# Sliding-window attention and an MLP on one core: two row blocks centred on ScalarE instead of VectorE, sums of W2 moved between periods, one transpose moved by a unit

## The chip, the core and the metric

The kernel runs on one core of a Trainium2 chip. Its engines work side by side, each through its own queue in order: TensorE (PE: matmuls and transposes, with weight loads as PEld), VectorE (DVE), ScalarE (ACT), GpSimd (POOL), and SyncE (SP), which here only issues transfers. The metric is the device time of one execution in microseconds (us); the runs shown before have a median of 311.74 us. "PSUM" is the memory that PE writes; it is handed out here in banks.

## What is computed

Eight batches, eight heads, 576 positions, head size 64. Attention looks back over 64 positions, and its output, put together over the heads (512 columns), goes through a layer norm, two matrix products with a relu between them, and a residual add:

```python
scores = scale * np.matmul(q, k.transpose(0, 1, 3, 2))
mask = (rel >= 0) & (rel < window)          # rel = row - column, window = 64
attn = softmax(np.where(mask, scores, -1e9))
x = matmul(attn, v), heads side by side      # (8, 576, 512)
xn = (x - mu) / np.sqrt(var + 1e-06) * g_ln
out = x + np.maximum(xn @ w_ch1, 0.0) @ w_ch2   # 512 x 2048, 2048 x 512
```

## The kernel before

**Groups.** The first 512 rows of each batch are a group (0 to 7) of four row blocks of 128; the last 64 rows of all batches make group 8. For each block the attention has these steps:

- `t_main` (L219) transposes q and k, on PE with a copy out of PSUM by ACT or DVE, from group 3 on q by a DMA of SP;
- `s_mm` (L260) multiplies them on PE and takes the exponential on ACT; `s_mask` (L295) applies the mask on DVE;
- `b_step` (L302) multiplies with v on PE (tile xps) and on DVE divides by the sum (L323, L326) and takes mean and variance (L328, L331); v is used in two alignments, vA and vB. From group 2 on vB is made by `make_vB` (L164) with two DMAs that POOL issues (L165, L166);
- `z_step` (L335) makes z, the centred block in half precision. For groups 0 and 1 it is called at the end of `b_step` and only subtracts the mean, on DVE (L341); the scale is applied after the MLP (`newton`, L367, and L417). For later groups POOL also applies the scale (L345 to L348);
- `zt_step` (L350) transposes z into zT, on PE with a copy by ACT (L360, L363) for groups 0 and 1 and for block 3 of groups 3 and 5, otherwise by a DMA of SP (L356).

**Periods and units.** The MLP of group g is one period of the loop at L823. `mlp_units` (L386) gives a list of units of PE work: first the product with W1 (`l1`, L392, 128x512 outputs, or `l1_half`, L526, half as wide), each ended by a relu on ACT, then the product with W2. In the periods of groups 0 and 1 the latter is done directly (`l2`, L403, four matmuls a unit, and in group 0 `l2_two`, L539, for its first two blocks), and `add_out` (L414) adds each finished block on DVE and stores it. The bank of such a block is one of two with the tag "mm", so the third block waits until the first has been added.

From group 2 on W2 is multiplied by Strassen's scheme in Winograd's form: seven products instead of eight (`product`, L450, in the order 1, 2, 6, 5, 7, 4, 3) of half-size blocks, into banks A, B and C. It needs four sums of the hidden activations in each period (`s_sums`, L435, DVE, tiles sS) and four sums of blocks of W2, made once (`w2_sums`, L705, DVE, tiles wT):

```python
o, x, y, op = {3: (t3, b22, b12, ALU.subtract), 2: (t2, t3, b11, ALU.add),
               4: (t4, b21, t2, ALU.subtract), 1: (b12, b12, b11, ALU.subtract)}[i]
nc.vector.tensor_tensor(out=o, in0=x, in1=y, op=op)
```

Number 1 overwrites the block b12 of W2 itself, so it must come behind group 1's products with W2 and behind T3. Each sum is called in two halves of 128x1024. `post` (L477) adds a bank to the block on DVE; product 6 goes on in bank A after product 1 has been added (L497), product 7 after that.

**The order.** It is written out by hand. `at(i, f, ...)` (L831) puts a step into slot i, and the step is issued behind unit i of the period; within a slot the order of the calls holds. Every engine runs its part of this list in order, so where a step stands sets what is queued behind it. Group g's period holds the attention of group g + 1: group 1's blocks 0 and 1 come in slots 18 and 21 of group 0's period (L850, L851), their transposes in slots 22 and 24 (L852, L853), which are the units of `l2_two` and the first of `l2`. The casts of W2 from f32 are POOL's (`w2_cast`, L203); they are issued before the loop and run as the loads land, some of which land in the tiles wT (L195). In group 1's period T3 stands in slots 25 and 28 (L881, L882), and in group 2's period T2, number 1 and T4 in slots 4 to 9 (L907 to L910), ahead of and among `b_step` of block 1 (slot 7), the mask of block 2 (slot 8) and the first halves of `s_sums` (slots 8 to 11).

Of the kernel before, what the change touches and what calls it, by code (L numbers as in the profile page):

```python
# [10 lines left out]
FP32 = mybir.dt.float32  # L11
# [3 lines left out]
AF = mybir.ActivationFunctionType  # L15
ALU = mybir.AluOpType
# [4 lines left out]
def kernel(  # L21
# [10 lines left out]
    nc = tc.nc  # L32
# [11 lines left out]
    scale = 1.0 / (D ** 0.5)  # L44
# [257 lines left out]
    def b_step(g, kb):  # L302
# [29 lines left out]
        if g < 2:  # L332
            z_step(g, kb)

    def z_step(g, kb):  # L335
        z = p_blk.tile([128, DM], FP16, tag="z", name=f"z_{g}_{kb}")
        zsd[(g, kb)] = z
        xv = x_norm[(g, kb // 2)][:, kb % 2, :]
        mu, var = mvg[g][:, kb, 0:1], mvg[g][:, kb, 1:2]
        if g < 2:  # L340
            nc.vector.tensor_scalar(out=z, in0=xv, scalar1=mu, scalar2=None, op0=ALU.subtract)  # L341
            return
        t = p_blk.tile([128, 3], FP32, tag="rsz", name=f"rsz_{g}_{kb}")
        ve, rs, nm = (t[:, i:i + 1] for i in range(3))
        nc.gpsimd.tensor_scalar(out=ve, in0=var, scalar1=1.0, scalar2=EPS, op0=ALU.mult, op1=ALU.add)  # L345
        nc.gpsimd.tensor_tensor(out=rs, in0=ve, in1=mhalf, op=ALU.pow)
        nc.gpsimd.tensor_scalar(out=nm, in0=mu, scalar1=rs, scalar2=-1.0, op0=ALU.mult, op1=ALU.mult)
        nc.gpsimd.tensor_scalar(out=z, in0=xv, scalar1=rs, scalar2=nm, op0=ALU.mult, op1=ALU.add)  # L348
# [474 lines left out]
    for g in range(NGRP):  # L823
        if g == NGRP - 1:
            for _ in rest:
                pass
            break
        units, s_sums = mlp_units(g, (8, 16)[g] if g < 2 else 0, g == 0, g > 1)
        slots = [[] for _ in range(len(units) + 1)]

        def at(i, f, *a):  # L831
            slots[min(i, len(slots) - 1)].append((f, a))

        b = g + 1
        if g == 0:
            at(0, b_step, 0, 3)
            at(1, zt_step, 0, 2)
            at(3, zt_step, 0, 3)
            at(4, newton, 0, 0, 4)
            at(11, t_main, 1, 0, 0, 1)  # L840
            at(12, t_main, 1, 1, 0, 1)
            at(13, vB_cur, 1, 0, 1)
            at(13, vB_prev, 1, 0, 1)
            at(13, vB_cur, 1, 1, 1)
            at(13, vB_prev, 1, 1, 1)
            at(16, s_mm, 1, 0)
            at(16, s_mask, 1, 0)
            at(17, s_mm, 1, 1)
            at(17, s_mask, 1, 1)
            at(18, b_step, 1, 0)  # L850
            at(21, b_step, 1, 1)  # L851
            at(22, zt_step, 1, 0)  # L852
            at(24, zt_step, 1, 1)  # L853
            at(26, t_main, 1, 0, 1, 0)
            at(27, t_main, 1, 1, 1, 1)
            at(28, vB_cur, 1, 2, 0)
            at(28, vB_prev, 1, 2, 1)
            at(29, vB_cur, 1, 3, 0)
            at(29, s_mm, 1, 2)
            at(29, s_mask, 1, 2)  # L860
            at(30, s_mm, 1, 3)
            at(30, s_mask, 1, 3)
            at(30, load_v, 2, 0, 4)
            at(33, b_step, 1, 2)
        if g == 1:
            at(0, cast_qk, 2, 0)
            at(0, cast_qk, 2, 1)
            at(1, b_step, 1, 3)
            at(2, zt_step, 1, 2)
            at(13, newton, 1, 0, 4)  # L870
            at(5, zt_step, 1, 3)
            at(4, alloc_v, 2)
            at(4, alloc_qkT, 2)
            at(4, alloc_vB, 2)
            at(5, cast_v, 2, 0, 4)
            at(5, make_vB, 2)
            at(4, t_main, 2, 0, 0)
            at(4, t_main, 2, 1, 0)
            at(6, t_main, 2, 0, 1)
            at(6, t_main, 2, 1, 1)  # L880
            at(25, w2_sums, 3, 0, 4)  # L881
            at(28, w2_sums, 3, 4, 8)  # L882
            for j in range(4):
                at((9, 13, 16, 19)[j], s_mm, 2, j)
                at((10, 14, 17, 20)[j], s_mask, 2, j)
                at((14, 17, 20, 23)[j], b_step, 2, j)
                at((14, 17, 20, 23)[j], z_step, 2, j)
                at((18, 21, 24, 27)[j], zt_step, 2, j)
            at(3, load_qk, 3, 0)
            at(4, load_qk, 3, 1)  # L890
            at(7, load_v, 3, 0, 4)
            at(8, alloc_qkT, 3)
            at(8, cast_qk, 3, 0)
            at(10, cast_qk, 3, 1)
            at(14, alloc_v, 3)
            at(14, cast_v, 3, 0, 2)
            at(14, cast_v, 3, 2, 4)
            at(17, alloc_vB, 3)
            at(17, make_vB, 3)
            at(31, s_mm, 3, 0)  # L900
            at(31, s_mask, 3, 0)
            for i, (x, half) in zip((12, 24, 12, 28), ((0, 0), (1, 0), (0, 1), (1, 1))):
                at(i, t_main, 3, x, half, 0)
            at(40, load_qk, 4, 0)
            at(40, load_qk, 4, 1)
            at(40, load_v, 4, 0, 4)
        if g == 2:  # L907
            for m, i in enumerate((2, 1, 4)):
                at(4 + 2 * m, w2_sums, i, 0, 4)
                at(5 + 2 * m, w2_sums, i, 4, 8)  # L910
        if g > 1 and g + 2 < B:
            at(11, alloc_qkT, g + 2)
            if g + 2 >= XQ:
                at(11, cast_qk, g + 2, 0, (0,))
                at(11, cast_qk, g + 2, 1, (0,))
                at(11, cast_qk, g + 2, 0, (1,))
            else:
                at(11, cast_qk, g + 2, 0)
        if g > 1 and b < B:
            for j in range(4):  # L920
                if j:
                    at((2, 7, 12)[j - 1], s_mm, b, j)
                    at((3, 8, 13)[j - 1], s_mask, b, j)
                at((2, 7, 12, 17)[j], b_step, b, j)
                at((2, 7, 12, 17)[j], z_step, b, j)
                at((12, 12, 18, 23 if b in (3, 5) else 22)[j], zt_step, b, j)
        for n, i in enumerate(TAILS.get(g, ())):
            ts = (10, 11, 14, 20) if n else (1, 2, 5, 11)
            at(ts[0], s_mm, NGRP - 1, i)
            at(ts[1], s_mask, NGRP - 1, i)  # L930
            at(ts[2], b_step, NGRP - 1, i)
            at(ts[2], z_step, NGRP - 1, i)
            at(ts[3], zt_step, NGRP - 1, i)
        n = g + 2
        if g > 1 and n < B:
            at(16, cast_qk, n, 1, (1,) if n >= XQ else (0, 1))
            at(20, alloc_v, n)
            at(20, cast_v, n, 0, 2)
            at(21, cast_v, n, 2, 4)
            at(21, alloc_vB, n)  # L940
            at(21, make_vB, n)
            for i, (x, half) in zip((13, 18, 13, 22) if g == 2 else (13, 17, 13, 21),
                                    ((0, 0), (1, 0), (0, 1), (1, 1))):
                at(i, t_main, n, x, half, 0)
            at(27, s_mm, n, 0)
            at(28, s_mask, n, 0)
            if n + 1 < B:
                at(40, load_qk, n + 1, 0)
                at(40, load_qk, n + 1, 1)
                at(40, load_v, n + 1, 0, 4)  # L950
        if g > 1:
            for i in range(1, 5):
                at(7 + i, s_sums, 0, 4, i)
                at(13 + i // 3, s_sums, 4, 6, i)
                at((15, 15, 19, 21)[i - 1], s_sums, 6, 8, i)
        for n, i in enumerate(TAILS.get(g + 1, ())):
            if n == 0:
                at(1, load_tail, i)
                at(24 if i < 2 else 18, cast_tail, i)
                at(27 if i < 2 else 22, t_tail, i, 0)  # L960
                at(29 if i < 2 else 22, t_tail, i, 1)
            else:
                at(25, load_tail, i)
        if len(TAILS.get(g, ())) == 2:
            at(3, cast_tail, TAILS[g][1])
            at(7, t_tail, TAILS[g][1], 0)
            at(8, t_tail, TAILS[g][1], 1)
        if g == NGRP - 2:
            at(0, w1_sums, 1, 2)
            at(3, w1_sums, 3)  # L970
            at(21, w1_sums, 4)
            at(24, z_sums, NGRP - 1, 1, 2)
            at(25, z_sums, NGRP - 1, 3, 4)
            at(27, begin_last)
        for i, u in enumerate(units):
            if g > 1 and i == 20:
                tbank["shared"] = True
            u()
            for f, a in slots[i]:
                f(*a)  # L980
        for f, a in slots[len(units)]:
            f(*a)
# [28 lines left out]
```

The softmax here doesn't subtract the row's maximum and nothing guards it: scores larger than these inputs give would overflow.

## Time and profile before

| | us |
|---|---|
| median of four runs | 311.74 |
| lowest and highest | 310.88, 312.64 |
| the profiled execution | 312.63 |
| its span, from the first instruction to the last | 310.8 |
| TensorE busy, POOL busy | 297.5, 171.5 |
| idle time of PE up to 46 us after its start, ended by: mask, two exponentials, casts of W1, a copy of zT | 2.3, 0.7, 0.6, 0.9 |

All starts below are counted in us from the beginning of the span. A timeline's line gives start, duration, engine, source line and operation, the tile written and the tiles read, shapes, how many instructions are merged into the line, and in brackets how long the engine had been idle before and which engine's work ended that wait. The group periods, by TensorE's first matmul with W1 in each: group 1 from 58.17, group 2 from 93.86, group 3 from 126.04, group 4 from 157.7. The granted TensorE clock is full speed (0.999) over the span.

### The profile page before, as it was taken

To read this page: it belongs to the slowest core of one execution; us is meant where nothing else is said; L and a number is where in the kernel's file an instruction comes from. 1 tells how busy PE (TensorE), PEld (TensorE's weight loads), DVE (VectorE), ACT (ScalarE), POOL (GpSimd) and SP (SyncE) were. 2 spreads that over 40 slices of the span, in tenths; PEclk is the share of its full clock that TensorE was granted. 3 is DMA by queue.
4 is the path that set the end of the run, shared out by engine and by line. 5 is a ranking of instruction groups with operands and counts; after the bars stand their busy time and mean duration, and the time that the engine had idled before them with its cause. 6 is when DMAs were issued, how large, how long until landed. Compare 5 with 4: busy or idle time off the path is not lost.

```text
span 310.8 us, 7624 instructions
## 1 busy us (share of the span) xinstructions
PE 297.5 (96%) x3089; PEld 198.2 (64%) x3089; DVE 219.6 (71%) x411; ACT 153.0 (49%) x258; POOL 171.5 (55%) x255
## 2 busy tenths in 40 slices
PE   7988989999999999999999989999999999999992
PEld 4556545697454578546854776459646855788882
DVE  0788585846766995589656945896569685777972
ACT  2576624587227732876167526762375048315500
POOL 7569676454952789279806964698246506204300
PEclk9999999999999999999999999999999999999999
DMA  8999999999777996898279997963690394003013
GB/s 190 264 389 287 329 353 265 269 293 241 152 178 221 244 176 130 273 285 109 44 219 316 198 152 219 313 140 70 201 183 17 54 198 142 2 0 137 0 37 101
DMA packets 109893, 57.43 MB, mean 185 GB/s; under 512 B 79841, under 2 KB 100833, under 8 KB 109858
## 3 DMA queue, kind: packets, MB, share of 16 engines
q1 hardware_dynamic: 108800, 53.75, 69.7%
q0 software_dynamic: 768, 2.80, 3.8%
q8 instruction: 24, 0.39, 0.5%
q10 hardware_dynamic: 290, 0.40, 0.4%
q14 instruction: 11, 0.09, 0.1%
HBM read 38.80 MB, written 9.44 MB: 155 GB/s over the span
## 4 chain that ended last, share of the span: by engine, by line
PE 72%; DMA 11%; DVE 5%; SPq 4%; POOL 4%; issue 2%; ACT 0%; POOLq 0%; ACTq 0%
PE hps L395 23%; PE pA L472 10%; PE pB L472 7%; PE pC L472 7%; PE ch L407 7%; PE hph L531 5%; DMA qk<-in_k_dram 4%; DMA wT<-in_moe_w_ch_dram 3%; PE xps L320 3%; PE sc L286 3%; PE lA L581 2%; DMA w1s<-in_moe_w_ch_dram 2%; SPq L141 2%; DVE sS L446 2%; PE tp L229 2%; DMA zT<-z 2%
## 5 line engine op out<-in xcount | busy, mean ns | idle before, releaser
L395 PE MATMUL hps<-zT,w1g 128*128 128x512 f16 x416 | 96.3, 380 | 0.0
L399 ACT ACTIVATE hrT<-hps 128x512 f16<-128x512 f32 x104 | 62.3, 599 | 38.6 <-PE hps L395 35.1
L395 PEld LDWEIGHTS <-w1g 128*128 128x128 f16 x416 | 38.3, 98 | 42.0 <-issue 0.9
L293 ACT ACTIVATE pt<-sc 128x512 f16<-128x512 f32 x72 | 39.0, 595 | 28.1 <-DVE xn L479 15.6
L472 PEld LDWEIGHTS <-sS 128*128 128x128 f16 x448 | 43.3, 98 | 5.4 <-issue 0.5
L345 POOL TENSOR_SCALAR rsz<-mvg 128x1 f32<-128x1 f32 x28 | 10.3, 369 | 59.4 <-DVE mvg L331 58.7
L128 POOL CAST qk<-qk 128x1024 f16<-128x1024 f32 x32 | 35.2, 1112 | 12.1 <-DMA qk<-in_q_dram 5.0
L472 PEld LDWEIGHTS <-hrT 128*128 128x128 f16 x336 | 32.4, 98 | 5.4 <-ACT hrT L620 0.3
L215 ACT COPY qkT<-tp 128x1024 f16<-128x1024 f16 x16 | 16.1, 1012 | 35.4 <-PE tp L229 31.1
L479 DVE TENSOR_TENSOR xn<-pA,xn 128x512 f32<-128x512 f32 x28 | 19.2, 685 | 18.5 <-PE pA L472 18.5
L300 DVE TENSOR_TENSOR pt<-pt,mask 128x1024 f16<-128x1024 f16 x32 | 25.0, 788 | 8.8 <-ACT pt L293 8.8
L348 POOL TENSOR_SCALAR z<-xn,rsz 128x512 f16<-128x512 f32 x28 | 25.0, 892 | 4.5 <-DMA zT<-z 1.6
L472 PE MATMUL pA<-wT,sS 128*128 128x256 f16 x224 | 26.9, 273 | 0.3 <-DVE xn L479 0.3
L472 PE MATMUL pC<-w2s,sS 128*128 128x256 f16 x224 | 26.9, 273 | 0.0
L326 DVE TENSOR_TENSOR xn<-xps,rcp 128x512 f32<-128x512 f32 x36 | 24.9, 691 | 1.5 <-DMA out_dram<-xn 0.3
L328 DVE BATCH_NORM_STATS2 stats<-xn 128x6 f32<-128x512 f32 x36 | 25.0, 695 | 1.2
L531 PE MATMUL hph<-zT,w1g 128*128 128x256 f16 x192 | 23.8, 273 | 1.7 <-ACT zT L363 0.9
L323 DVE RECIPROCAL rcp<-xps 128x8 f32<-128x8 f32 x36 | 7.3, 204 | 25.4 <-PE xps L320 25.4
L446 DVE TENSOR_TENSOR sS<-hrT 128x512 f16<-128x512 f16 (+1 forms) x40 | 24.5, 612 | 0.6 <-ACT hrT L399 0.6
L407 PE MATMUL ch<-w2s,hrT 128*128 128x512 f16 x96 | 22.9, 380 | 0.0
L531 PEld LDWEIGHTS <-w1g 128*128 128x128 f16 x192 | 17.9, 98 | 4.8 <-POOL w1g L190 1.4
L147 POOL CAST vA<-v 128x1024 f16<-128x1024 f32 (+2 forms) x19 | 17.2, 928 | 6.6 <-DMA v<-in_v_dram 6.6
(109 smaller groups left out, 448.4 us busy)
## 6 DMA issues: line engine op xcount, KB each, us to landing
out_dram<-xn SPq DMA_DIRECT2D x33, 256.0 KB, 2.9
qk<-in_q_dram SPq DMA_DIRECT2D x16, 512.0 KB, 6.1
qk<-in_k_dram SPq DMA_DIRECT2D x16, 512.0 KB, 7.0
v<-in_v_dram SPq DMA_DIRECT2D x32, 256.0 KB, 6.8
w2s<-in_moe_w_ch_dram SPq DMA_DIRECT2D x9, 512.0 KB, 9.6
w1s<-in_moe_w_ch_dram SPq DMA_DIRECT2D x4, 512.0 KB, 7.5
tk<-in_k_dram SPq DMA_DIRECT2D x8, 256.0 KB, 4.6
tv<-in_v_dram SPq DMA_DIRECT2D x8, 256.0 KB, 5.3
```

Source lines behind the costliest of these rows:

```text
L128: nc.gpsimd.tensor_copy(out=dst[:, :].rearrange("p (a j) e d -> p a e j d", j=j), in_=t[:, :].rearrange("p (a e j d) -> p a e j d", e=2, j ...
L293: nc.scalar.activation(out=o, in_=i, func=AF.Exp, bias=0.0, scale=scale)
L300: nc.vector.tensor_tensor(out=ptv, in0=ptv, in1=mb, op=ALU.mult)
L326: nc.vector.tensor_tensor(out=xn, in0=xps[:, :, 0:D], in1=rcp_b, op=ALU.mult)
L328: nc.vector.bn_stats(out=stats, in_=xv)
L348: nc.gpsimd.tensor_scalar(out=z, in0=xv, scalar1=rs, scalar2=nm, op0=ALU.mult, op1=ALU.add)
L395: nc.tensor.matmul(out=hps, lhsT=w1g[:, kc, 128 * hc:128 * (hc + 1)], rhs=zT[g][:, kc, :], start=(kc == 0), stop=(kc == NKC - 1),)
L399: nc.scalar.activation(out=hrT[:, hc, :], in_=hps, func=AF.Relu, bias=0.0, scale=1.0)
L407: nc.tensor.matmul(out=ch[kb], lhsT=hrT[:, hc, 128 * kb:128 * (kb + 1)], rhs=w2s[:, hc, :], start=(hc == 0), stop=(hc == NHC - 1),)
L446: nc.vector.tensor_tensor(out=o, in0=x, in1=y, op=op)
L472: nc.tensor.matmul(out=o, lhsT=a[:, c, 128 * p:128 * p + 128], rhs=wv[:, c, :], start=(first and (p == 0 or split_c) and c == 0), stop=(c ...
L531: nc.tensor.matmul(out=hps[:, e], lhsT=w1g[:, kc, 128 * hc:128 * (hc + 1)], rhs=zT[g][:, kc, 256 * half:256 * half + 256], start=(kc == 0) ...
```

## The change

Three edits. `z_step`: for blocks 0 and 1 of group 1 DVE no longer makes z; it only negates the mean into a 128x1 tile, and ACT makes z as identity(x + bias) with that tile as the bias. The tile comes from the ring "rsz" that later groups' `z_step` uses. `zt_step` of group 1's block 1 moves from slot 24 to slot 25 of group 0's period. The sums of W2: T3 moves from slots 25 and 28 of group 1's period to slots 7 and 8, T2 from group 2's period to slots 25 and 28 of group 1's; in group 2's period number 1 and T4 move up into slots 4 to 7.

```diff
         if g < 2:
-            nc.vector.tensor_scalar(out=z, in0=xv, scalar1=mu, scalar2=None, op0=ALU.subtract)
+            if g == 0 or kb > 1:
+                nc.vector.tensor_scalar(out=z, in0=xv, scalar1=mu, scalar2=None, op0=ALU.subtract)
+            else:
+                nmu = p_blk.tile([128, 3], FP32, tag="rsz", name=f"nmu_{g}_{kb}")[:, 0:1]
+                nc.vector.tensor_scalar(out=nmu, in0=mu, scalar1=-1.0, scalar2=None, op0=ALU.mult)
+                nc.scalar.activation(out=z, in_=xv, func=AF.Identity, bias=nmu, scale=1.0)
             return
...
             at(22, zt_step, 1, 0)
-            at(24, zt_step, 1, 1)
+            at(25, zt_step, 1, 1)
...
-            at(25, w2_sums, 3, 0, 4)
-            at(28, w2_sums, 3, 4, 8)
+            at(7, w2_sums, 3, 0, 4)
+            at(8, w2_sums, 3, 4, 8)
+            at(25, w2_sums, 2, 0, 4)
+            at(28, w2_sums, 2, 4, 8)
...
         if g == 2:
-            for m, i in enumerate((2, 1, 4)):
+            for m, i in enumerate((1, 4)):
                 at(4 + 2 * m, w2_sums, i, 0, 4)
                 at(5 + 2 * m, w2_sums, i, 4, 8)
```

The two lines with 7 and 25 stand in the block `if g == 1`. On SP and POOL the order of the instructions stays the same. On PE only the four transposes of block 1 change places with four matmuls; on ACT the two new operations stand ahead of the copies of zT of blocks 0 and 1.

## Prediction

> **What bounds the kernel now.** I read the busy shares first, then TensorE's waits behind the start-up, then the timelines around each of those waits. Times are us from the span's start.
>
> The page's engine shares:
>
> ```profile
> PE 297.5 (96%) x3089; PEld 198.2 (64%) x3089; DVE 219.6 (71%) x411; ACT 153.0 (49%) x258; POOL 171.5 (55%) x255
> ```
>
> PE is busy for 297.5 of 310.8, and the change takes no matmul away. So it can only win PE's idle time. The waits of PE between 46 and 200 (engine and line, what it waited for: total, times, longest):
>
> ```profile
> PE ztp L360 <- POOL z L348: 1.1, 1, 1.1
> PE ch L546 <- POOL w2s L204: 0.8, 1, 0.8
> PE pA L472 <- DVE xn L479: 0.3, 1, 0.3
> PE ztp L360 <- POOL vA L135: 0.2, 1, 0.2
> ```
>
> Four waits, 2.4 us. The first is at 183.51, in the period of group 4, which the diff doesn't touch. The other three, at 46.09, 115.13 and 119.46, are where it could act. The timeline of each engine at the first of them:
>
> ```profile
> 44.65 0.49 DVE L341 TENSOR_SCALAR z<-xn,mvg 128x512 f16<-128x512 f32 x1
> ...
> 44.83 1.21 POOL L204 CAST w2s<-wT 128x1024 f16<-128x1024 f32 x1 [1.04 <-DMA wT<-in_moe_w_ch_dram]
> 46.08 1.04 POOL L204 CAST w2s<-w2s 128x1024 f16<-128x1024 f32 x1
> ...
> 46.09 1.02 PE L546 MATMUL ch<-w2s,hrT 128*128 128x512 f16 x4 [0.84 <-POOL w2s L204]
> ...
> 47.81 1.61 DVE L417 SCALAR_TENSOR_TENSOR xn<-ch,rstdg,xn 128x512 f32<-128x512 f32 x2
> ```
>
> The cast that releases PE takes 1.21 beside z of block 0, and the next one, without z beside it, 1.04. The other two waits hang on VectorE's queue in the period of group 2:
>
> ```profile
> 102.23 0.21 DVE L323 RECIPROCAL rcp<-xps 128x8 f32<-128x8 f32 x1 [0.28 <-PE xps L320]
> ...
> 104.03 0.66 DVE L712 TENSOR_TENSOR wT<-w2s,wT 128x1024 f16<-128x1024 f16 x1
> 104.60 0.68 DVE L300 TENSOR_TENSOR pt<-pt,mask 128x1024 f16<-128x1024 f16 x1
> ...
> 105.81 0.69 DVE L712 TENSOR_TENSOR wT<-w2s,wT 128x1024 f16<-128x1024 f16 x1
> ...
> 114.39 0.68 DVE L479 TENSOR_TENSOR xn<-pA,xn 128x512 f32<-128x512 f32 x1
> ...
> 115.13 1.91 PE L472 MATMUL pA<-wT,sS 128*128 128x256 f16 x16 [0.34 <-DVE xn L479]
> ```
>
> From 102.23 on DVE has no idle time; it reaches the add of bank A (L479) only at 114.39, and product 6, which goes on in that bank, waits 0.34 for it. Block 3 of the next group (xps, stats, then z on POOL) stands behind this add on DVE, so ztp at 119.46 waits 0.23 more.
>
> **The change, part by part.**
>
> **W2 sums.** DVE's order changes; the number of sums and all matmuls stay, and none of these steps issues a DMA. In the period of group 2 the two halves of T4, at 104.03 and 105.81, move up to where the differences of b12 stood (100.66), because T2 is gone from 99.46. DVE is then free at about 101.9, and block 1's reciprocal at 102.23 is released by PE, so nothing is late there. Behind it 2 x 0.60 (the pitch from one such row to the next) = 1.2 us disappear. How much arrives at the add is read from the period of group 4, which has the same queue without sums: reciprocal at 165.91, add at 177.32, 11.41 us; here it is 114.39 - 102.23 = 12.16. So the add comes 0.75 sooner, at 113.64, and ends at 114.32; PE is ready at 115.13 - 0.34 = 114.79. **Gain 0.34**, with 0.47 in hand. Then z of block 3: it ended at 118.25 + 1.02 = 119.27, and with VectorE 0.75 sooner ends at 118.52; PE would be there at 119.46 - 0.23 - 0.34 = 118.89. **Gain 0.23**, with 0.37 in hand. Bounds for the two together: 0 (the queue is held elsewhere) to 0.57 (there is no more to win); I take 0.57, as group 4's period is the same work.
>
> In the period of group 1, T2 stands where T3 stood (87.80 and 90.40, 1.06 and 0.91), same shapes. T3 goes behind the copy of k's transpose, which ends at 68.45, and before the mask at 71.44, which waits on ScalarE: 2.99 us of idle time for 2 x 0.57 (alone, as at 104.03) to 2 x 1.06 (beside POOL, as at 87.80) = 1.1 to 2.1 us. Cost 0; without that cover the mask, and with it xps at 75.11, would have 3 us in hand still.
>
> **Centring on ScalarE.** Off DVE go two z of 0.49; on come two negations of 128x1, not in the trace: between the 0.16 of a 128x4 row (L379) and the 0.49 of z itself, nearest the first, 0.17. ScalarE gets two operations on 128x512, f32 in, f16 out: between 0.57 (vB cast, 64x512) and 1.01 (128x1024 copy), nearest the 0.60 of the relu, which is the same size. ScalarE is idle from 41.8 to 47.38, so block 0 is free of charge. Block 1: statistics end at 47.17, negation 47.38, z about 48.05, against 47.70 before. Queued behind it on ScalarE is the copy of block 0's zT (47.38 becomes 48.05); its first reader is hph at 58.17 and its bank is wanted at 50.42, so 1.8 us are in hand.
>
> What it gives is on POOL: without z beside it the cast takes 1.04, not 1.21, and ends 0.17 sooner, and PE with it. Bounds 0 (the landing of the weights moves) to 0.17.
>
> A page prices the operation higher: the Trainium skill, "ScalarE: Activation LUTs", What ACT_TABLE_LOAD costs, gives an activation with a pointer bias 280 ns + 0.833 ns an element, by which z would be an estimated 0.71. No activation with such a bias is in the trace. Block 1 would be ready at 48.16 and the sum would stay as it is.
>
> **The transpose a unit later.** PE's order around it was ch (to 48.47), ztp of block 1 (0.23), then eight matmuls of ch of the third block, from 48.70. Those take the bank of the first block, which add_out frees (L417, the first of the two, 47.81 + 0.75 = 48.56). Now they come first: with the 0.17 PE is there at 48.30, add_out starts at 47.64 (released by PE's matmul) and ends at 48.39, ch starts at 48.43. Four matmuls (0.86) and ztp (0.23) later the next four start at 49.52, against 48.70 + 0.86 = 49.56 before. So of the 0.17 a **gain of 0.04** is left. Bounds: if the cast gains nothing, ch starts at 48.60 and the four after it at 49.69, a loss of 0.13; if add_out is no bar, a gain of 0.17.
>
> **Sum.** 0.34 + 0.23 + 0.04 = 0.61, between -0.13 and 0.74. From 119.46 to 183.51 PE has no other wait. The wait at 183.51 runs back, by the chain of waits, over z's transpose (landing 5.02 after 177.51) and POOL to xps at 165.49 on PE, so it should move along unshortened. The profiled execution took 312.63 (span 310.8 and 1.8 around it): 312.02. It lies 0.89 above the median 311.74, so the prediction on the median is **311.1**.
>
> **Against the change** speaks one observation: POOL's first vB issue, beside the copy of k's transpose on DVE, takes 0.74 at 67.34, and 0.59 at 85.05. T3 now comes right behind that copy. The second issue (68.09 to 68.61) meets its start; it isn't needed before block 1's xps at 78.64.
>
> [...]
>
> **Rivals.**
>
> **A, the sum holds: 311.1.** Its own range by the bounds is 311.0 to 311.9.
>
> **B, the gain is absorbed at 183.51: 311.7.** z there waits for a transpose that SP issues only when its loads are out, at 177.51. If those loads go by the DMA engines' pace and not by PE's, PE arrives 0.6 sooner and waits 1.7. For it: SP issued loads without a break from 160.45 to 177.35. Against it: they start behind an output store at 159.96, which VectorE's adds release.
>
> **C, that wait goes too: 311.74 - 0.61 - 1.10 = 310.0.** POOL's work is no longer held by DVE between 104 and 108 (z of block 1 there took 1.61, 0.76 alone), and SP's transposes could run ahead for a period. For it: z at 182.70 was late by a transfer and not by work. Against it: the loads in front of that transfer.
>
> **D, slower: T3 meets vB's first issue.** vB of group 2 is issued at 67.34 and lands 7.6 later, at 74.94; its xps starts at 75.11, so 0.1 to 0.2 us are in hand. The issue follows the cast of v, which follows the landing of v at 65.1. Should v land 1.1 us later (issue at 68.45 or after), T3's halves go ahead of the issue: 2 x 1.06 less 0.15, a stall of about 2.0 on PE, net 0.61 - 2.0 = 1.4 slower: 313.1. Against it: the order as traced has 1.1 us to spare.
>
> That DVE's queue doesn't shorten (the operations of 108 to 114 being held by POOL's three casts, 3.68 us from 109.06) gives 0.04 less or none of the sum: B's time too; group 4's period speaks against it, since its casts lie the same way.
>
> **How the numbers follow.** A 0.62, B with the unshortened queue 0.14, C 0.14, D 0.10. About 0.5% (1.56 us) is what a measurement of this kernel can tell from no change. Beyond it lie C (1.71) and a tail of A, 0.18 together, and half of D, 0.06; the rest, 0.76, is within it. The range takes in A, B and C with 0.4 us for the spread of the medians below C (the runs before span 1.8 us), and above it adds to B the 0.9 by which the highest run lies over the median: 309.6 to 312.7. D, 0.10, is left out.
>
> **What would show it.** Right: no wait of PE before product 6 of group 2's period and none before the ztp behind it; the cast that ends PE's wait near 46 at 1.04; VectorE idle before block 2's reciprocal near 107. Wrong: a wait at xps of group 2's block 0 near 75 (D); the wait of 1.1 at 183 grown to 1.7 (B) or gone (C); a wait of ch behind add_out near 48.4 of more than 0.2.

## The result and the profile after

| | before | after |
|---|---|---|
| median, us | 311.68 | 311.0 |
| lowest of the runs | 310.64 | 310.18 |
| ratio, 95% interval | | 0.9974 [0.9964, 0.9983] |
| profiled execution, its span | 312.63, 310.8 | 311.46, 309.7 |

0.26% of 311.68 is 0.81 us (0.53 to 1.12); the medians alone lie 0.68 apart. Forecast were 0.61 and 311.1. The agreement of the total is better than that of its parts.

The shares of the engines after the change:

```profile
PE 297.9 (96%) x3089; PEld 198.1 (64%) x3089; DVE 220.7 (71%) x411; ACT 154.3 (50%) x260; POOL 170.9 (55%) x255
```

PE does the same work. Its waits between 46 and the end:

```profile
PE xps L320 <- DMA vB<-vA: 0.7, 1, 0.7
PE ztp L365 <- ACT qkT L215: 0.2, 1, 0.2
```

Of the four waits of before, those near 46, before product 6 and near 183 are gone, that of the ztp in group 2's period is still there with another releaser, and one is new. VectorE and PE in group 2's period, whose lines answer to those from 102.23 to 115.13 of before:

```profile
102.73 0.21 DVE L323 RECIPROCAL rcp<-xps 128x8 f32<-128x8 f32 x1 [0.28 <-PE xps L320]
...
107.87 0.21 DVE L323 RECIPROCAL rcp<-xps 128x8 f32<-128x8 f32 x1 [0.15 <-PE xps L320]
...
114.14 0.68 DVE L484 TENSOR_TENSOR xn<-pA,xn 128x512 f32<-128x512 f32 x1
...
115.13 1.91 PE L477 MATMUL pA<-wT,sS 128*128 128x256 f16 x16
```

No sum of W2 stands behind 102.73 any more, VectorE waits for PE again at 107.87, and the add comes 114.14 - 102.73 = 11.41 after the reciprocal, to the hundredth what group 4's period had. Product 6 has no wait. Near 46 ScalarE makes z, and POOL's cast beside it takes 1.04 (ScalarE, then POOL):

```profile
44.76 0.72 ACT L346 ACTIVATE z<-xn,nmu 128x512 f16<-128x512 f32 x1 [3.18 <-DVE nmu L345]
```

```profile
45.51 1.04 POOL L204 CAST w2s<-w2s 128x1024 f16<-128x1024 f32 x1 [0.66 <-DMA w2s<-in_moe_w_ch_dram]
```

To see where PE gains and loses I laid the start of each of its 3089 matmuls beside the same one of before. The difference (after minus before) runs: -0.85 at the matmuls that wait for the cast near 46, -0.34 at the fifth matmul of the third block, past the transpose of group 1's block 1, +0.48 from xps at 75.6, -0.01 from product 6 (a step of 0.51), -1.27 from the ztp near 183, -1.19 at the end. A single pair of executions thus mixes what the edits do with what transfers do. So the experiments were read in two ways: by time, and by such steps, over twelve further profiles. Diffs are against before, from "The transpose back in slot 24" on against after.

### The profile page after: what moved, and what is told of

It is laid out like the page before. It is cut to its first block, busy times and chain, and to the rows that moved or that the text cites. A ratio compares the mean times of both kernels' runs of the same rounds, so it can differ in the third digit from the quotient of the medians.

```text
span 309.7 us, 7628 instructions
## 1 busy us (share of the span) xinstructions
PE 297.9 (96%) x3089; PEld 198.1 (64%) x3089; DVE 220.7 (71%) x411; ACT 154.3 (50%) x260; POOL 170.9 (55%) x255
## 4 chain that ended last, share of the span: by engine, by line
PE 75%; DMA 13%; SPq 6%; DVE 2%; POOL 1%; issue 1%; ACT 0%; POOLq 0%
PE hps L400 28%; PE pA L477 12%; PE pB L477 8%; PE pC L477 8%; PE ch L412 6%; DMA qk<-in_k_dram 4%; SPq L141 4%; PE xps L320 4%; DMA wT<-in_moe_w_ch_dram 3%; PE sc L286 3%; DMA vB<-vA 3%; PE lA L586 2%; PE tp L229 2%; DMA v<-in_v_dram 2%; DMA w1s<-in_moe_w_ch_dram 2%; SPq L89 1%
## 5 line engine op out<-in xcount | busy, mean ns | idle before, releaser
L400 PEld LDWEIGHTS <-w1g 128*128 128x128 f16 x416 | 38.3, 98 | 42.0 <-issue 0.7
L300 DVE TENSOR_TENSOR pt<-pt,mask 128x1024 f16<-128x1024 f16 x32 | 26.5, 833 | 7.0 <-ACT pt L293 7.0
L320 PEld LDWEIGHTS <-pt 128*64 128x64 f16 x576 | 12.2, 110 | 14.5 <-issue 6.1
```

Source lines behind the costliest of these rows:

```text
L300: nc.vector.tensor_tensor(out=ptv, in0=ptv, in1=mb, op=ALU.mult)
L320: nc.tensor.matmul(out=xps[64 * r:64 * r + 64, h, :D + 1], lhsT=pt[:, par, hp, r, :], rhs=rhs, start=True, stop=True)
L400: nc.tensor.matmul(out=hps, lhsT=w1g[:, kc, 128 * hc:128 * (hc + 1)], rhs=zT[g][:, kc, :], start=(kc == 0), stop=(kc == NKC - 1),)
```

## The experiments

"ch" is the tile of a product with W2. The theory is the prediction's: the sums of W2 make most of the gain, the centring and the transpose together next to nothing. Rivals: the centring makes it; the gain is the wait near 183 going (C); T3 costs what the sums bring (D).

Steps of PE in all profiles, us from start to start. "Block 1": from the last ch matmuls that wait on a cast of W2 to the fifth matmul of the third block, over the transpose (2.38 of work alone). "Product 6": from 113.9 of before to product 6 (0.76 alone). "xps": over the start of group 2's block 0 (0.21 alone). "183": wait of the ztp there. The ratio is that of the times to before.

| kernel | z by | slot | block 1 | xps | product 6 | 183 | ratio, 95% interval |
|---|---|---|---|---|---|---|---|
| before | DVE | 24 | 2.38 | 0.21 | 1.27 | 1.3 | |
| before, again | DVE | 24 | 3.59 | 0.21 | 1.27 | 0 | |
| sums only | DVE | 24 | 2.67 | 0.21 | 0.76 | 0 | 0.9998 [0.9968, 1.0028] |
| sums only, again | DVE | 24 | 2.62 | 0.21 | 0.76 | 0 | |
| casts on ScalarE | DVE | 24 | 2.38 | 0.21 | 1.27 | 0 | 1.0046 [1.0016, 1.0075] |
| z strided | DVE | 24 | 3.59 | 0.20 | 1.27 | 0.1 | 1.0040 [1.0014, 1.0066] |
| centring only | ACT | 24 | 2.41 | 0.21 | 1.27 | 1.7 | 0.9979 [0.9960, 0.9997] |
| centring and slot | ACT | 25 | 2.87 | 0.21 | 1.27 | 0 | 0.9979 [0.9957, 1.0001] |
| after | ACT | 25 | 2.62 | 0.97 | 0.76 | 0 | 0.9974 [0.9964, 0.9983] |
| after, again | ACT | 25 | 2.52 | 0.21 | 0.76 | 0 | |
| slot undone | ACT | 24 | 2.38 | 0.36 | 0.76 | 0 | 0.9984 [0.9961, 1.0007] |
| T3 in group 0 | ACT | 24 | 2.38 | 0.21 | 0.76 | 0 | 0.9989 [0.9965, 1.0013] |
| v sooner | ACT | 24 | 2.38 | 0.21 | 0.76 | 0 | 0.9978 [0.9954, 1.0002] |
| T3 and newton later | ACT | 25 | 2.52 | 2.03 | 0.76 | 0.2 | 1.0105 [1.0064, 1.0146] |

### The sums alone

```diff
-            at(25, w2_sums, 3, 0, 4)
-            at(28, w2_sums, 3, 4, 8)
+            at(7, w2_sums, 3, 0, 4)
+            at(8, w2_sums, 3, 4, 8)
+            at(25, w2_sums, 2, 0, 4)
+            at(28, w2_sums, 2, 4, 8)
...
-            for m, i in enumerate((2, 1, 4)):
+            for m, i in enumerate((1, 4)):
```

> Before with only the sums of W2 moved (T3 to slots 7 and 8, T2 to 25 and 28, the others up); z and the transpose as before. Theory (the sums make the gain): the wait of PE before product 6 of group 2's period, 0.51 us from start to start, is gone, z of group 3's block 3 is ready sooner, PE's ztp there still waits for the copy by ScalarE; the time is 0.5 lower, a ratio near 0.998, and the same gain as in after. Rival (T3 in the period of group 1 costs what the sums bring): T3 beside POOL's transfers takes 4 to 5 us, vB of group 2 lands late, PE waits some 0.7 at its xps and the time is unchanged, 1.000. Second rival (the gain is the wait of 1.27 at 183 going): gone here too if the sums are its cause, 0.995; still there if not.

> The kernel with only the sums moved, for a second profile; its times had a tail to 316.8. Theory: the wait before product 6 is gone again (0.51). If this execution is a late one, z on VectorE has been shut out near 45 and 48 (1.2 to 1.3 each), PE is 1 to 1.5 late there, or T3 at slots 7 and 8 takes 4 us or more and the mask of group 2's block 0 and PE's xps behind it come late. If it is a short one (311), nothing new is learnt on the tail.

The step at product 6 is 0.76 in both profiles, and in all eight with the sums moved, and 1.27 in all six without: 0.51 belongs to the sums. It reaches the end: from product 6 to TensorE's last matmul all fourteen profiles take 188.36 to 188.44, the step near 183 left out, so what is won at product 6 is not lost behind it, and PE's differences from execution to execution arise ahead of product 6 or near 183. The time doesn't show the 0.51: 0.9998 with an interval of 0.6%, although the medians are 311.12 and 312.10. Five of the twelve runs took 312.3 to 316.9, the others 310.4 to 311.2, and both profiled executions were short ones (spans 308.5 and 308.4). What happens in the long ones no profile shows.

### The centring alone, and with the transpose moved

```diff
-            nc.vector.tensor_scalar(out=z, in0=xv, scalar1=mu, scalar2=None, op0=ALU.subtract)
+            if g == 0 or kb > 1:
+                nc.vector.tensor_scalar(out=z, in0=xv, scalar1=mu, scalar2=None, op0=ALU.subtract)
+            else:
+                nmu = p_blk.tile([128, 3], FP32, tag="rsz", name=f"nmu_{g}_{kb}")[:, 0:1]
+                nc.vector.tensor_scalar(out=nmu, in0=mu, scalar1=-1.0, scalar2=None, op0=ALU.mult)
+                nc.scalar.activation(out=z, in_=xv, func=AF.Identity, bias=nmu, scale=1.0)
```

> Before with only the centring of group 1's blocks 0 and 1 on ScalarE; the transpose stays in slot 24, the sums stay. Theory: the wait before product 6 (0.51) stays; the cast of W2 that releases PE near 46 takes 1.04 and not 1.21; the transpose of block 1 finds its z ready (statistics end at 47.1, z at about 48.2 with an operation of 0.72, PE there at 48.3); time 0 to 0.2 lower, ratio 0.9995 to 1.000. Rival (the ScalarE part makes the gain): 0.997 to 0.998. Rival (z comes late without the move): PE waits up to 0.2 before the transpose, ratio 1.000 to 1.001.

> Before with the centring on ScalarE and the transpose in slot 25, the sums as before. Theory: as the centring alone, and ch of the third block waits 0.1 to 0.25 for the add of the first block, so within 0.15 of the centring alone; wait of 0.51 before product 6 stays; ratio 0.9995 to 1.0005. Rival (these two edits and not the sums make the gain): 0.997 to 0.998.

Both are 0.21% under before, which is what the rival said of them and four times the theory's bound; by time the rival fits better. The interval of the first excludes no change, that of the second just doesn't. The wait before product 6 is there in both, as the theory had it. The profile of the centring alone is of its longest run (312.64), with 1.7 lost near 183.

### Before, a second profile

> The kernel before, unchanged, for a second profile. Theory: the wait of 0.51 before product 6 and the 0.40 before the ztp behind it come back to the hundredth, since they hang on VectorE's and ScalarE's queues; the landing of the weights near 45 moves by some tenths. Whether the 1.27 before the ztp at 183 comes back says whether it belongs to the order of the work (then it is there in every run of before) or to the pace of the transfers in one execution.

The waits before product 6 and the ztp came back, the 1.27 near 183 didn't. And this execution lost at block 1 what the first had not (VectorE, then POOL, then PE):

```profile
44.97 1.27 DVE L341 TENSOR_SCALAR z<-xn,mvg 128x512 f16<-128x512 f32 x1
46.16 0.19 DVE L323 RECIPROCAL rcp<-xps 128x8 f32<-128x8 f32 x1
...
48.06 1.30 DVE L341 TENSOR_SCALAR z<-xn,mvg 128x512 f16<-128x512 f32 x1
49.29 1.39 DVE L417 SCALAR_TENSOR_TENSOR xn<-ch,rstdg,xn 128x512 f32<-128x512 f32 x2
```

```profile
44.92 1.04 POOL L204 CAST w2s<-wT 128x1024 f16<-128x1024 f32 x1 [0.60 <-DMA wT<-in_moe_w_ch_dram]
...
48.04 1.04 POOL L128 CAST qk<-qk 128x1024 f16<-128x1024 f32 x1 [0.75 <-PE ch L546]
```

```profile
49.42 0.40 PE L360 MATMUL ztp<-ident,z 128*128 128x128 f16 x4 [0.62 <-DVE z L341]
50.08 1.24 PE L407 MATMUL ch<-w2s,hrT 128*128 128x512 f16 x5 [0.26 <-DVE xn L417]
```

In the first profile of before z began at 44.65, the cast at 44.83, and the cast was stretched to 1.21. Here the cast begins 0.05 ahead of z and takes its 1.04, and z takes 1.27 instead of 0.49; the same again at 48.04 and 48.06. PE then waits for z and for the add behind it: 3.59 - 2.38 = 1.21 us. Which of the two begins first hangs on the landing of the weights, which moved by over 1 us between the profiles.

The other profiles show the same. In the five with z as in before there are seven rows near 45 and 48 in which z and a cast overlap. The four z that began during a cast ended 0.28 behind its end, whether they took 0.52, 0.64, 1.27 or 1.30; the three casts that began during z ended 0.90 behind z's end and took 1.21 to 1.26.

### Taking POOL's casts away from z

```diff
+    def w2_cast_act(i):
+        nc.scalar.copy(out=w2s[:, 2 * i:2 * i + 2, :], in_=wst.pop(("w2", i)))
...
-        w2_cast(i)
+        if i < 6:
+            w2_cast(i)
...
+            at(20, w2_cast_act, 6)
+            at(21, w2_cast_act, 7)
```

> Before (z on VectorE, sums and transpose as before) with the casts 6 and 7 of W2 on ScalarE in slots 20 and 21 instead of on POOL, so that POOL does nothing that could exclude VectorE while z of group 1's blocks 0 and 1 is made; the number of operations stays. Theory (z and POOL's casts exclude each other; in some executions z goes first and the cast is 0.2 longer, in others the cast goes first and z takes 1.27 and 1.30, and PE loses 1.4 to 1.5 at the transpose and at ch): z takes 0.49 twice, no wait of PE before the transpose of block 1, and the time falls as with the centring on ScalarE, ratio 0.997 to 0.999. Rival (the centring wins by taking work off VectorE, whatever POOL does): ratio 1.000. The casts on ScalarE take about 1.0.

In the profile z takes 0.49 twice and block 1 is 2.38, as expected; the time is 0.46% up, against the theory and its rival alike. The profiled execution was the shortest of the twelve (311.57), so what the others lost is not shown, and the run can't decide between the two.

```diff
-            nc.vector.tensor_scalar(out=z, in0=xv, scalar1=mu, scalar2=None, op0=ALU.subtract)
+            if g == 0 or kb > 1:
+                nc.vector.tensor_scalar(out=z, in0=xv, scalar1=mu, scalar2=None, op0=ALU.subtract)
+            else:
+                nc.vector.tensor_scalar(out=z[:, :].rearrange("p (h d) -> p d h", h=H), in0=xv.rearrange("p (h d) -> p d h", h=H),
+                                        scalar1=mu, scalar2=None, op0=ALU.subtract)
```

Here z of group 1's blocks 0 and 1 stays on VectorE, but is read and written with the head index innermost, a step of 64 elements. "Fast form" below means z in its usual order; the question is whether the order decides that z and the casts shut each other out.

> [...] Theory (the centring wins because a fast-form z and POOL's casts shut each other out, z then taking 1.27 and 1.30 in some executions and the cast 0.2 more in others): z takes about 0.7 in every execution whatever POOL does, the casts beside it 1.04, no wait of PE above 0.2 at the transpose of block 1, ratio 0.997 to 0.999 as with the centring on ScalarE. Rival (VectorE is simply freed by the centring): z of 0.7 instead of 0.49 makes VectorE later by 0.4, ratio 1.000 to 1.002. If a strided z still takes 1.2 or more beside a cast, the form is not what decides.

VectorE, then POOL:

```profile
44.35 2.24 DVE L344 TENSOR_SCALAR z<-xn,mvg 128x512 f16<-128x512 f32 x1
...
48.32 1.37 DVE L344 TENSOR_SCALAR z<-xn,mvg 128x512 f16<-128x512 f32 x1
```

```profile
44.38 1.04 POOL L204 CAST w2s<-wT 128x1024 f16<-128x1024 f32 x1 [0.95 <-DMA wT<-in_moe_w_ch_dram]
45.66 1.81 POOL L204 CAST w2s<-w2s 128x1024 f16<-128x1024 f32 x1 [0.24 <-DMA w2s<-in_moe_w_ch_dram]
```

The strided z is no 0.7: 2.24 and 1.37. It ended 1.17 and 1.18 behind the cast that ran beside its start, and the casts that began during it took 1.81 and 1.28 instead of 1.04. So the strided z and the casts shut each other out as well: by what was set down beforehand the order is not what decides, and this kernel can't tell theory from rival. It shows the other half: z later on VectorE is time on PE. Block 1 is 3.59, and the time 0.40% up, 1.2 us.

### The transpose back in slot 24

```diff
-            at(25, zt_step, 1, 1)
+            at(24, zt_step, 1, 1)
```

> After with the transpose of group 1's block 1 back in slot 24. Theory: ScalarE has z ready at about 48.2 where PE comes at about 48.0 to 48.3, so PE waits 0 to 0.25 there and then has ch without a wait, against the 0.24 that ch waits in after: the same within 0.1 us, ratio to before 0.997 to 0.998. Rival (the move protects PE in the executions in which z is late): 0.3 or more slower than after, ratio 0.998 to 1.000.

Block 1 is 2.38 here and 2.38 to 2.41 in the three other kernels with the centring and slot 24, against 2.52 to 2.87 in the four profiles with slot 25: the move costs 0.14 to 0.49, where ch waits for the add of the first block. The time can't tell it from after.

### After, a second profile, and T3 elsewhere

> The changed kernel as it is, for a second profile. Theory: no wait before product 6, the wait of 0.40 before the ztp behind it as in the first profile; T3 anything from 1.2 to 5 us, by how POOL's casts lie; the wait at xps of group 2's block 0 follows the landing of v and vB and not T3; the 1.27 before the ztp at 183 may be there or not.

T3 in the first profile of after (VectorE, then POOL):

```profile
66.94 1.22 DVE L217 COPY qkT<-tp 128x1024 f16<-128x1024 f16 x1 [1.57 <-PE tp L229]
68.08 4.60 DVE L717 TENSOR_TENSOR wT<-w2s 128x1024 f16<-128x1024 f16 x2
72.61 0.68 DVE L300 TENSOR_TENSOR pt<-pt,mask 128x1024 f16<-128x1024 f16 x1
```

```profile
68.36 0.53 POOL L166 DMA_DIRECT2D vB<-vA  x1
68.88 0.33 POOL L208 MEMSET qkT<- 128x256 f16 x1
69.13 3.00 POOL L128 CAST qk<-qk 128x1024 f16<-128x1024 f32 x3
```

The second half stood through three casts without a gap between them. It began at 68.68, 0.45 ahead of the first of them, and was held all the same; why is not shown. In the second profile T3 took 2.17, in every other kernel with T3 moved 2.12. Beside T3 the second issue of vB takes what it took in before (0.53). The wait at xps in the first profile comes from elsewhere, as its chain of waits shows (start, us, what):

```profile
60.22 5.05 DMA v<-in_v_dram
...
65.41 1.90 POOL vA L147
67.31 0.29 issue
67.61 7.85 DMA vB<-vA
75.46 0.14 issue
75.59 0.45 PE xps L320 x16
```

v landed 0.3 later than in before, vB took 0.25 longer, and PE was 0.3 sooner. T3 isn't in the chain.

```diff
-            at(13, newton, 1, 0, 4)
+            at(17, newton, 1, 0, 4)
...
-            at(7, w2_sums, 3, 0, 4)
-            at(8, w2_sums, 3, 4, 8)
+            at(11, w2_sums, 3, 0, 4)
+            at(12, w2_sums, 3, 4, 8)
```

> After with T3 in slots 11 and 12 of group 1's period instead of 7 and 8, and newton in slot 17 instead of 13, so that T3 comes when POOL's issue of vB and its casts are through. Theory (T3 in slots 7 and 8 costs what POOL's casts make it wait, up to 4.6 us, and in some executions it delays what follows): T3 takes 1.2 to 2 us, ratio to before 0.996 to 0.997, a little under after. Rival (the wait at xps of group 2's block 0 is the landing of v and not T3): T3 is short and that wait comes and goes as before, ratio 0.997 to 0.998 like after.

1.05% slower. Of the 4.5 us in its profile, 1.8 are a late vB (v was cast at 67.82, 2.7 later than in before), and 2.45 come from what I moved along with T3, newton, which met POOL's casts of v:

```profile
81.48 0.16 DVE L389 TENSOR_TENSOR rstdg<-rstdg,rstmp 128x4 f32<-128x4 f32 x1
81.68 0.62 DVE L386 TENSOR_TENSOR rstmp<-rstdg 128x4 f32<-128x4 f32 x1
82.33 1.03 DVE L387 TENSOR_TENSOR rstmp<-rstmp 128x4 f32<-128x4 f32 x1
83.39 0.96 DVE L388 TENSOR_SCALAR rstmp<-rstmp 128x4 f32<-128x4 f32 x1
```

```profile
82.31 2.01 POOL L147 CAST vA<-v 128x1024 f16<-128x1024 f32 x2
```

Operations on four columns, 0.16 to 0.19 elsewhere in the row, take up to 1.03 while POOL casts, and the mask behind them keeps PE's next xps waiting. So this run says nothing on T3 and much on POOL.

```diff
-            at(25, zt_step, 1, 1)
+            at(24, zt_step, 1, 1)
...
+            at(25, w2_sums, 3, 0, 4)
+            at(25, w2_sums, 3, 4, 8)
...
-            at(7, w2_sums, 3, 0, 4)
-            at(8, w2_sums, 3, 4, 8)
```

The added lines stand in group 0's period.

> After with the transpose back in slot 24 and T3 in slot 25 of group 0's period, where VectorE is idle between 49.4 and 52.0, instead of slots 7 and 8 of group 1's. Theory (T3 costs where it stands between POOL's work and the masks): here POOL casts q, k and v too, T3 takes 1.2 to 2.5, and what follows on VectorE is the copy of k's transpose near 52 which PE needs at 53.7; time as the kernel with slots 7 and 8 and slot 24, ratio 0.997 to 0.999. Rival (every delay of a cast of v or of the copy of k here moves the loads of v for group 2, and with them vB): PE's wait at xps near 75 grows by 0.5 to 2, ratio above 1.000.

T3 takes 2.12 here too, nothing behind it is late in the profile, and the time is that of slot 24 with T3 in slots 7 and 8.

### The loads of v sooner

```diff
-            at(25, zt_step, 1, 1)
+            at(24, zt_step, 1, 1)
...
-            at(28, vB_cur, 1, 2, 0)
-            at(28, vB_prev, 1, 2, 1)
-            at(29, vB_cur, 1, 3, 0)
+            at(25, vB_cur, 1, 2, 0)
+            at(25, vB_prev, 1, 2, 1)
+            at(25, vB_cur, 1, 3, 0)
...
-            at(30, load_v, 2, 0, 4)
+            at(27, load_v, 2, 0, 4)
```

> After with the transpose back in slot 24, and the reads of group 1's v for vB moved from slots 28 and 29 to 25 of group 0's period, the loads of group 2's v from slot 30 to 27, ahead of one output store. Theory (the wait at xps of group 2's block 0, near 75, which was 0.75 in after, is the landing of v, then its cast, then the transfer vB in 7.6 to 7.9): v lands some 0.5 to 1 sooner, the wait is gone in every execution, ratio 0.995 to 0.997. Rival (the loads go by the pace of the transfers and not by their issue): v lands as before, ratio 0.997 to 0.999 like after.

v is cast 0.4 sooner than in before in an execution in which PE was 0.7 later, so 1.1 sooner against PE, and xps has no wait. The time, 0.9978, is no better than after's. No version here is shown to beat after.

## Why the prediction was right in its total, and where it was wrong

The total came out 0.1 from the forecast, in part by luck: product 6 gave 0.17 more than its term, the ztp behind it nothing, the centring more than its bound and the moved transpose cost more. Of the signs that the prediction named, three of the four for being right are there (no wait before product 6, the cast at 1.04, VectorE idle at 107.87), and so are all three for being wrong: a wait at xps near 75 (0.75), the wait near 183 gone, and ch waiting 0.24 behind the add near 48. The first two of these three come and go between executions of one kernel.

**The wait before product 6: right, and larger than priced.** The mechanism held in all eight profiles with the sums moved, and the reading of group 4's period held to the hundredth in after. The term 0.34 should have been 0.51. The idle time in brackets is counted from the modelled end of the last matmul (1.04 for eight); the next starts 0.87 after the eight began, and the 0.17 between is lost too.

**The ztp behind it, 0.23: wrong.** z was ready sooner (119.01; 119.27 before; counted from the reciprocal of block 1 it is 0.76 sooner, where 0.75 was predicted), and PE waited the same. In after's lines (POOL, ACT, PE):

```profile
117.99 1.02 POOL L353 TENSOR_SCALAR z<-xn,rsz 128x512 f16<-128x512 f32 x1
```

```profile
118.39 1.01 ACT L215 COPY qkT<-tp 128x1024 f16<-128x1024 f16 x1 [2.87 <-PE tp L229]
```

```profile
119.46 0.38 PE L365 MATMUL ztp<-ident,z 128*128 128x128 f16 x4 [0.23 <-ACT qkT L215]
```

And in before's (POOL, ACT):

```profile
118.25 1.02 POOL L348 TENSOR_SCALAR z<-xn,rsz 128x512 f16<-128x512 f32 x1
119.21 0.24 POOL L135 MEMSET vA<- 128x32 f16 x1
```

```profile
118.40 1.01 ACT L215 COPY qkT<-tp 128x1024 f16<-128x1024 f16 x1 [3.38 <-PE tp L229]
```

From slot 20 on the transposes share one bank, and the copy of k's transpose out of it ended at 119.40, in before (119.41) as here. The prediction read the wait as one for z. But z had ended 0.14 before that copy; the profile named POOL's fill of vA (L135), which ended within 0.04 of the copy, and I didn't look for the other. The copy follows PE's own transpose of k (tp), so a shorter queue of VectorE could not win this wait.

**The centring, 0.17 at most: wrong in size.** One execution showed z ahead of the cast, the cheap order. In the other order z itself is shut out, twice, and PE loses 1.21; I priced only the direction that the row showed. The Trainium skill, "SBUF — State Buffer", SBUF: two separate sides, says of the ports that VectorE, in some of its operations, shares with GpSimd that whichever starts first has them for the whole instruction, while the other is blocked. The seven rows of z agree (0.28 and 0.90 behind the other's end); T3's second half and the first strided z, which by their starts in the trace were first (by 0.45 and 0.03) and were held, do not. Of the five profiles with z as in before, two lost nothing (in one of them two casts were taken off POOL), two 0.24 and 0.29, one 1.21; with the centring and slot 24 four of four lost at most 0.03. The time of the centring alone is 0.21% lower (0.03 to 0.40%). That z is shut out is shown; that this makes all of the centring's gain is argued, since the two kernels that were to separate it from a VectorE that is simply freed failed to.

**The transpose a unit later: right in direction, priced too low.** It costs 0.14 to 0.49 by the steps; 0.13 was put to it.

**T3 at no cost: right in the profiles, wrong in size.** It took 2.12 to 4.60, where 1.1 to 2.1 were worked out. It delays nothing that PE waits for: from the fifth matmul of the third block to the last matmul before xps PE takes 25.35 to 25.60 in the six profiles with T3 in slots 7 and 8, and 25.35 to 25.83 in the six without the sums moved. The sums' 0.51 us is 0.16%, with the centring's 0.21% together 0.37%, where after's time has 0.26% (0.17 to 0.36). The moved transpose takes 0.14 to 0.49 us of that back, and the centring's interval alone (0.03 to 0.40%) covers the difference, so no loss by T3 is shown. What makes the long runs of the sums alone, up to 316.9, stays open.

**The rivals.** B, the gain absorbed near 183, didn't occur: in none of the eight profiles with the sums moved does the ztp there wait more than 0.2. C's wait did go in after, but it is missing in a second run of before as well and present with the centring alone, so 2 of 6 profiles without the sums have it at over 1 us and 0 of 8 with them: by this the sums aren't shown to remove it. D's place was right, its cause not: in the first profile of after v landed 0.3 later and vB took 0.25 longer, with T3 not in the chain.

**ScalarE's operation** took 0.72, not the 0.60 of the nearest row. The estimate from the Trainium skill, "ScalarE: Activation LUTs", What ACT_TABLE_LOAD costs, was 0.71, and the runs agree with it. In the profiles with slot 24 at most 0.03 was lost at block 1 with it.

## What to carry to other kernels

Where VectorE and POOL both work near a step that PE waits for, price both orders of the two and not only the one that a single trace shows: here 0.05 us decided between a cast longer by 0.2 and PE later by 1.2. A wait that a profile puts down to one engine may have a second condition ending within a tenth of a microsecond of it, so look for everything that the instruction needs before counting it as won. And take a wait's size from start to start of the waiting engine's instructions.

## What the runs showed of the hardware that I had not expected

POOL's casts can shut VectorE out for far longer than one of them lasts when they follow each other without a gap: a sum of 0.6 us took 4.0, though it began 0.45 ahead of the first cast. They do so to operations on four columns as well (1.03 against 0.16). Not every operation is shut out: in the fourteen profiles 60 rows of the statistics on the same block and 77 of the multiplication out of PSUM stand inside a cast, and all took 0.69 to 0.70. Reading and writing z with a step of 64 elements took VectorE 1.37 and 2.24 beside casts; as it went on for 1.17 and 1.18 behind the cast, an estimated 1.2 of that at least is its own, where z in order takes 0.49.
